# When the 64-bit weights of a gated layer are decoded: blocks moved between attention, expert 0 and experts 1 to 5

## The chip, the core and the metric

One core of a Trainium2 chip runs the whole program in one launch: attention, a mixture of experts, a gated feed-forward layer. The metric is the time of the launch in microseconds on the device. Three runs of the kernel before took 854.21, 855.8 and 856.52 us; the median is 855.8.

## The reference

For 4 batches of 8 heads, 576 positions and 64 columns a head, causal attention with a bias from running sums of `s`; its output, 2304 tokens of 512, goes to a top-1 mixture of eight experts (512 to 1024 to 512, relu), and that to an RMS norm and a gated layer of width 1536, all in float32 but for three weights:

```python
logits = x @ w_gate                      # mixture: one expert a token
h = np.maximum(xe @ w1[e], 0.0); ye = h @ w2[e]
out[mask] = gate_w[mask, None] * ye
xn = x / rms * rms_g                     # gated layer
g = xn @ w_gate                          # w_gate, w_val, w_out are float64
return ((g / (1 + np.exp(-g))) * (xn @ w_val) @ w_out).astype(np.float32)
```

The three weights of the gated layer reach the chip as 64-bit floats, 12 blocks (f = 0 to 11) of 128 x 512 words each. No engine reads them: a block is loaded as pairs of 32-bit words and decoded with shifts and masks.

## The kernel before

TensorE, VectorE, ScalarE and SyncE's DMA queue run in an order that the program writes out; each engine takes its instructions one after the other and waits on semaphores. GpSimd's order in attention and in the experts is the scheduler's.

**Attention** (`attention`). 16 head pairs p go through S (scores), X (exp), T (transposes), V (times values), W (copies to vp) and O (output and routing logits). All are laid into a plan by a time, ten units a pair, and emitted in the order of these times; other work has times of its own. After a batch (four pairs) `route` picks the expert of each token in some forty steps: VectorE finds the one-hot oh, TensorE ranks the tokens (rk), GpSimd scatters rows to xs with five indirect DMAs. The empty `yield 1` steps in it only let time pass in the plan.

**Weights of experts.** A float32 weight is split in a high part (a cast, `split` L728, ScalarE, or VectorE with `by_v`) and the rest (a subtraction; L743 on GpSimd for expert 0, L754 on VectorE for the others, one split late, `rest`). An expert has eight pieces of 512 KB, loaded by `feed` into one ring of four buffers (`staging`), through which the 64-bit blocks go as well. Expert 0's eight are split in attention at the times `PIECES`.

**Decoding** (`decoding` L1207) has five steps: shift, or, clear the sign (VectorE with `eng`, ScalarE's Abs without), scale, shift and or: L1212, L1213, L1214 or L1215, L1216, L1217. Of w_out, blocks 4 to 9 are decoded in attention (`out_load`, `out_first`, `out_last`, `out_keep`, the last storing 32-bit words to `wo32` in HBM), blocks 10 and 11 in expert 0 (`moe` L1007, into the one buffer `dw`). Of w_gate and w_val, blocks 0 and 1 are decoded in `glu_head`, a generator whose steps stand between the blocks of experts 6 and 7; the others in the gated layer.

**Experts** (`moe`). Expert s has eight blocks f of a first product (L891; h is written by ScalarE L894, its rest by VectorE L895), then four column blocks c of a second (L914), three passes each. Between them stand splits for the next expert, the turning of its rows (x_transpose), the norm of the expert before (`finish`) and the stores. In expert 0 the last batch's route runs on (`rank`).

**The gated layer** (`glu`, `glu_rest`), from 437 us on, is bound by TensorE and is not changed but for where its first blocks come from.

Of the kernel before, what the change touches and what calls it, by code (L numbers as in the profile page):

```python
# [19 lines left out]
E = 8  # L20
# [447 lines left out]
def route(k, b):  # L468
    nc, R = k.nc, k.rpool
    yield 1  # L470
    xt, lp = k.xt, k.lp
    sh = (128, 5, E)

    def t3(nm, dt=F32):
        return R.tile([128, 5, E], dt, name=f"{nm}{b}", tag=nm)

    def t2(nm, dt=F32):
        return R.tile([128, 5], dt, name=f"{nm}{b}", tag=nm)

    def up(x):  # L480
        return x.unsqueeze(2).broadcast_to(sh)

    w8 = k.w8.unsqueeze(1).broadcast_to(sh)
    base = k.base.unsqueeze(1).broadcast_to(sh)
    V = nc.vector
    lg, eq, dl, ex, ob, r1 = (t3(n) for n in ("lg", "eq", "dl", "ex", "ob", "r1"))
    mx, km, se, bt, rs = (t2(n) for n in ("mx", "km", "se", "bt", "rs"))
    oh, ix = t3("oh", BF16), t2("ix", U32)
    yield 1
    V.tensor_reduce(lg, lp, axis=AX.X, op=ALU.add)  # L490
    yield 1
    V.tensor_reduce(mx, lg, axis=AX.X, op=ALU.max)
    yield 1
    V.tensor_tensor(eq, lg, up(mx), op=ALU.is_ge)
    yield 1
    V.tensor_tensor(dl, lg, up(mx), op=ALU.subtract)
    yield 1
    V.tensor_tensor(eq, eq, k.w8v, op=ALU.mult)
    nc.scalar.activation(ex, dl, AF.Exp)
    yield 1  # L500
    V.tensor_reduce(km, eq, axis=AX.X, op=ALU.max)
    yield 1
    V.tensor_tensor(oh, up(km), w8, op=ALU.is_equal)
    yield 1
    for _ in range(3 if b < B - 1 else 0):
        yield 1
    ps = k.psum.tile([128, 48], F32, name=f"rk{b}", tag="b")
    rk = ps[:, 0:40].rearrange("p (t e) -> p t e", t=5)
    nc.tensor.matmul(rk, k.tri, oh, start=True, stop=False)
    for t in range(4):  # L510
        nc.tensor.matmul(rk[:, t + 1:5, :], k.ones, oh[:, t:t + 1, :].broadcast_to((128, 4 - t, E)), start=False, stop=t == 3)
    for t in range(5):
        nc.tensor.matmul(ps[:, 40:48], k.ones, oh[:, t, :], start=t == 0, stop=t == 4)
    yield 1
    V.tensor_tensor(ob, oh, base, op=ALU.mult)
    yield 1
    V.tensor_reduce(bt, ob, axis=AX.X, op=ALU.add)
    yield 1
    V.tensor_reduce(se, ex, axis=AX.X, op=ALU.add)
    yield 1  # L520
    V.tensor_scalar(xt[:, :, DM], k.tid, float(b * S), None, op0=ALU.add)
    yield 1
    V.tensor_scalar(se, se, 1e-9, None, op0=ALU.add)
    yield 1
    V.reciprocal(xt[:, :, DM + 1], se)
    yield 1
    V.tensor_tensor(r1, rk, oh, op=ALU.mult)
    yield 1
    V.tensor_reduce(rs, r1, axis=AX.X, op=ALU.add)
    yield 1  # L530
    V.tensor_tensor(ix, bt, rs, op=ALU.add)
    yield 1
    V.tensor_tensor(k.base, ps[:, 40:48], k.base, op=ALU.add)
    yield 1
    for t in range(5):
        n = 128 if t < 4 else 64
        yield 1
        i = nc.gpsimd.indirect_dma_start(
            out=k.xs, out_offset=bass.IndirectOffsetOnAxis(ap=ix[0:n, t:t + 1], axis=0),
            in_=xt[0:n, t, :], in_offset=None,  # L540
        )
        of_rows(k, "placed", in_turn(k, i).ins, k.filled)
        k.placed.append(i.ins)
    if b == B - 2:
        V.tensor_scalar(k.na, k.base[0:1, 0:1], float(NA), None, op0=ALU.min)
        V.tensor_scalar(k.base[:, 0:1], k.base[:, 0:1], float(NA), None, op0=ALU.max)
    if b == B - 1:
        for _ in order_experts(k):
            yield 1
# [73 lines left out]
MASK = -9.7  # L623
ROUTE = (35.2, 0.22)
FR = 2
PIECES = (81.8, 84.0, 91.8, 94.0, 159.0, 161.7, 165.3, 167.1)
EARLY_AT = (152.2, 165.25, 170.2, 170.3)
EARLY_P, EARLY_OUT = 9, 6
FILL = (12.6, 12.7, 12.8, 22.6, 22.7, 22.8, 32.5, 32.6)


def attention(k):
    k.st, k.todo, k.turn, k.half_done = {}, [], [], None
    with ExitStack() as es:
# [46 lines left out]
        for n in range(EARLY_OUT):  # L681
            at = 10 * (EARLY_P + n)
            add(at - (1.6, 5.0)[n] if n < 2 else at - 5.8, out_load, k, 4 + n)
            add(at + 6.3, out_first, k, 4 + n, k.nc.vector)
            add(at + 14.0, out_last, k, 4 + n)
            add(at + 16.4, out_keep, k, 4 + n)
        for n in (EARLY_OUT - 2, EARLY_OUT - 1):
# [12 lines left out]
        k.turn = []  # L700


RSTEPS = 40


PLACE = ((6, 7, 4, 5), (0, 1, 2, 3))
# [12 lines left out]
def feed(k, n=1):  # L719
    for _ in range(n):  # L720
        if k.order:
            s, u, q = k.order.pop(0)
            raw = staging(k, [2, 512], F32)
            src = (k.w1, k.w2)[u // 2]
            src = src[0, u % 2] if s == 0 else src[bass.ds(who(k, s), 1), u % 2].rearrange("e p q n -> (e p) q n")
            k.nc.sync.dma_start(out=raw, in_=src[:, q:q + 2, :])
            k.staged.append((s, u, q, raw))


def split(k, n=1, refill=True, by_v=False):  # L730
    nc = k.nc
    for _ in range(n):
        if k.staged:
            s, u, q, raw = k.staged.pop(0)
            if q == 0:
                new_unit(k, s, u)
            w = k.wt[s, u][:, q:q + 2]
            if by_v:
                nc.vector.tensor_copy(w[:, :, 0, :], raw)
            else:  # L740
                nc.scalar.copy(w[:, :, 0, :], raw)  # L741
            if s == 0:
                in_turn(k, nc.gpsimd.tensor_tensor(w[:, :, 1, :], raw, w[:, :, 0, :].bitcast(F32), op=ALU.subtract))  # L743
            else:
                rest(k)
                k.half_done = (w, raw)
            if refill:
                feed(k)
# [10 lines left out]
    k.early[f] = raw_load(k, 2, f)  # L759


def out_first(k, f, eng=None):
    for step in decoding(k, k.early[f], eng=eng)[0:3]:
        step()


def out_last(k, f, pool=None):
    if pool:
        done = k.early[-1] = pool.tile([128, 2 * CM], U32, name=f"dw{f}", tag="sq")[:, 0:512]
    else:  # L770
        done = k.early[-1] = new_raw(k).rearrange("p d two -> p (d two)")[:, 0:512]
    for step in decoding(k, k.early.pop(f), done)[3:5]:
        step()


def out_keep(k, f):
    k.nc.sync.dma_start(out=k.wo32[f // 2 - 2][:, f % 2, :], in_=k.early[-1].bitcast(F32))


STG = 4  # L780
# [207 lines left out]
def moe(k, close):  # L988
# [4 lines left out]
            next(k.last, None)  # L993

    k.order = [(s, u, q) for s in range(1, E) for u in range(4) for q in (0, 2)]
    late = range(4 + EARLY_OUT, NF)
    for f in late:
        out_load(k, f)
    row = ids(k, k.x[0], EARLY)
    keep_ids(k, row, 0)  # L1000
    rank(RANK[0])
    for f in range(8):
        gemm1(k, 0, f, NA)
        rank(RANK[f + 1])
        if f == 3:
            load_late(k)
        if f > 2 and f < 7:  # L1007
            (out_first, out_last)[f % 2 - 1](k, late[(f - 3) // 2], *((), (k.mpool,))[f % 2 - 1])
        if f > 4 and f % 2:
            out_keep(k, late[(f - 5) // 2])  # L1010
    load_x(k, 1)
    feed(k, STG - 1)
    first = tiles_of(CAP[0])
# [34 lines left out]
    for s in range(1, E):  # L1048
# [22 lines left out]
            next(head, None)  # L1071
        for c in range(4):
            gemm2(k, s, c, n)
            if c == 1:
                split(k)
            if not last:
# [156 lines left out]


def w_parts(k, f):
    return [k.raw[f, m].bitcast(F32)[:, :, n] for m in range(2) for n in (1, 0)]


# [92 lines left out]
def glu_head(k):  # L1331
# [3 lines left out]

    V, G = k.nc.vector, k.nc.gpsimd
    k.raw, k.ps = {}, {}
    w_load(k, 0, 0)
    yield
    w_load(k, 0, 1)  # L1340
    yield
    w_load(k, 1, 0)
    dec(0, 0, 0)
    yield
    w_load(k, 1, 1)
    dec(0, 0, 1)
    for g in range(2):
        glu_load(k, g)
    yield
    dec(0, 0, 2)  # L1350
    yield
    dec(0, 0, 3)
    yield
    dec(0, 0, 4)
    yield
    w_cast(k, 0, 0)
    dec(0, 1, 0, 1)
    yield
    w_rest(k, 0, 0, G)
    dec(0, 1, 2)  # L1360
    yield
    dec(0, 1, 3, 4)
    yield
    for n in (1, 4):
        w_cast(k, 0, n)
    yield
    for n in (1, 4):
        w_rest(k, 0, n, G)
    yield
    x_cast(k, 0, "A11")  # L1370
    x_rest(k, 0, "A11", V)
    dec(1, 0, 0, 1)
    yield
    x_cast(k, 0, "A12")
    dec(1, 0, 2)
    x_rest(k, 0, "A12", V)
    dec(1, 0, 3, 4)
    yield
    x_cast(k, 0, "A21")
    x_rest(k, 0, "A21", V)  # L1380
    dec(1, 1, 0, 1)
    yield
    x_cast(k, 0, "A22")
    x_rest(k, 0, "A22", G)
    dec(1, 1, 2, 3, 4)
    yield


# [548 lines left out]
def block_kernel(ctx, tc, q, kk, v, s, w_gate, w1, w2, wg, wv, wo, rms_g, out):  # L1937
# [7 lines left out]
    k.tokd = k.dpool.tile([YCOL], F32, name="tokd")  # L1945
    k.hd = k.dpool.tile([NG, 128, NF, GT], F32, name="hd")
    k.cumd = k.dpool.tile([32, S], F32, name="cumd")
    k.wo32 = k.dpool.tile([NF // 2 - 2, 128, 2, 512], F32, name="wo32")
    k.psum = ctx.enter_context(tc.tile_pool(name="psa", bufs=8, space=bass.MemoryType.PSUM))
    k.w64 = (k.wg, k.wv, k.wo64)  # L1950
# [82 lines left out]
```

## Time and profile before

| | |
|---|---|
| median of three runs | 855.8 us (854.21 to 856.52) |
| the profiled execution | 860.85 us |
| its span, first to last instruction | 859.1 us |
| TensorE busy | 827.8 us, 96% |
| VectorE / ScalarE / GpSimd busy | 637.5 / 462.2 / 232.4 us |
| mean granted clock of TensorE | 0.989 |
| moved by DMA | 145.67 MB |

PE is TensorE's matmuls, PEld its weight loads, DVE VectorE, ACT ScalarE, POOL GpSimd, SPq SyncE's queue. Times of rows are from the span's start. The number in brackets at the end of a row is how long the engine stood idle before it, and who ended that. A clock of 1.00 is TensorE's upper level, 2.4 GHz, 0.50 the lower, 1.2 GHz. Attention takes the span to about 194 us, expert 0 to 242, experts 1 to 7 to 437, the gated layer the rest.

### The profile page before, as it was taken

To read this page: it belongs to the slowest core of one execution; us is meant where nothing else is said; L and a number is where in the kernel's file an instruction comes from. 1 tells how busy PE (TensorE), PEld (TensorE's weight loads), DVE (VectorE), ACT (ScalarE), POOL (GpSimd) and SP (SyncE) were. 2 spreads that over 40 slices of the span, in tenths; PEclk is the share of its full clock that TensorE was granted. 3 is DMA by queue.
4 is the path that set the end of the run, shared out by engine and by line. 5 is a ranking of instruction groups with operands and counts; after the bars stand their busy time and mean duration, and the time that the engine had idled before them with its cause. 6 is when DMAs were issued, how large, how long until landed. Compare 5 with 4: busy or idle time off the path is not lost.

```text
span 859.1 us, 15794 instructions
## 1 busy us (share of the span) xinstructions
PE 827.8 (96%) x5622; PEld 754.6 (88%) x5622; DVE 637.5 (74%) x1424; ACT 462.2 (54%) x1059; POOL 232.4 (27%) x251
## 2 busy tenths in 40 slices
PE   7999999988999999999999999999999999999994
PEld 4767666667899999999999999999999997899994
DVE  6657587956575567567789998888888968867881
ACT  6988888872656556566453434333333335454340
POOL 3425745262000000000130313444444443022120
PEclk9999999998999999999999999999999999999998
DMA  7999978262674665666645342333323264544510
GB/s 227 309 302 300 296 244 265 93 216 93 202 237 153 185 196 167 211 187 197 212 159 175 107 166 77 114 105 105 105 95 108 92 257 150 152 147 130 163 54 29
DMA packets 79324, 145.67 MB, mean 170 GB/s; under 512 B 7376, under 2 KB 44267, under 8 KB 79235
## 3 DMA queue, kind: packets, MB, share of 16 engines
q1 hardware_dynamic: 76275, 135.03, 50.1%
q0 software_dynamic: 2912, 9.46, 2.9%
q8 instruction: 46, 0.75, 0.4%
q14 instruction: 43, 0.35, 0.1%
q10 hardware_dynamic: 48, 0.07, 0.0%
HBM read 107.52 MB, written 37.02 MB: 168 GB/s over the span
## 4 chain that ended last, share of the span: by engine, by line
PE 86%; DVE 5%; DMA 3%; ACT 2%; issue 1%; POOL 1%; SPq 0%; POOLq 0%; DVEq 0%; ACTq 0%
PE gg L1285 30%; PE g L914 12%; PE gp L1750 10%; PE g L891 9%; PE go L1685 6%; PE s L307 4%; PE t L370 4%; PE pvy L416 4%; PE tl L444 2%; DMA in<-cumd 1%; PE sm L338 1%; PE xp L862 1%; DMA raw<-in_w 1%; PE r L963 1%; PE r L952 1%
## 5 line engine op out<-in xcount | busy, mean ns | idle before, releaser
L914 PE MATMUL g<-h,u 128*128 128x256 f32 (+7 forms) x768 | 110.5, 303 | 5.0 <-DVE h L895 4.7
L914 PEld LDWEIGHTS g<-h,u 128*128 128x128 f32 x768 | 105.6, 196 | 6.6 <-DVE h L895 5.6
L891 PE MATMUL g<-xt,u 128*128 128x256 f32 (+7 forms) x768 | 104.5, 295 | 0.0
L891 PEld LDWEIGHTS g<-xt,u 128*128 128x128 f32 x768 | 101.6, 189 | 0.9
L1262 POOL TENSOR_TENSOR ws<-raw,ws 128x512 fp32r<-128x512 f32 (+1 forms) x25 | 33.5, 1352 | 232.2 <-ACT ws L1257 232.2
L351 ACT ACTIVATE p<-sc,nm 128x128 f32<-128x128 f32 (+3 forms) x128 | 71.2, 580 | 6.7 <-DVE nm L295 6.7
L754 DVE TENSOR_TENSOR u<-raw,u 128x1024 fp32r<-128x1024 f32 x56 | 68.0, 1216 | 0.4 <-ACT u L741 0.4
L1285 PE MATMUL gg<-gx2a,ws 128*128 128x384 f32 x360 | 67.4, 335 | 0.6 <-DVE tmp L1307 0.6
L1285 PE MATMUL gg<-gx0a,ws 128*128 128x384 f32 x360 | 67.7, 336 | 0.0
L741 ACT CAST u<-raw 128x1024 fp32r<-128x1024 f32 x62 | 65.1, 1050 | 4.7 <-DMA raw<-in_w 2.4
L1285 PE MATMUL gg<-gx1a,ws 128*128 128x384 f32 x360 | 67.1, 335 | 0.0
L1285 PEld LDWEIGHTS gg<-gx2a,ws 128*128 128x128 f32 x360 | 62.8, 188 | 0.9 <-DVE tmp L1307 0.9
L1285 PEld LDWEIGHTS gg<-gx0a,ws 128*128 128x128 f32 x360 | 63.1, 188 | 0.0
L1285 PEld LDWEIGHTS gg<-gx1a,ws 128*128 128x128 f32 x360 | 62.7, 188 | 0.0
L1323 POOL TENSOR_TENSOR hs<-tmp,hs 128x384 f32<-128x384 f32 x27 | 30.3, 1124 | 106.2 <-ACT hs L1321 106.2
L403 ACT COPY pt<-t 128x512 f32<-128x512 f32 (+3 forms) x160 | 55.7, 454 | 3.0 <-PE t L370 2.2
L370 PE MATMUL t<-ident,p 128*128 128x128 f32 x400 | 52.1, 275 | 0.1
L370 PEld LDWEIGHTS t<-ident,p 128*128 128x128 f32 x400 | 44.5, 140 | 8.3 <-DVE nm L295 8.0
L1671 POOL DMA_INDIRECT out<-raw,oid x18 | 20.5, 1140 | 112.1 <-DVE raw L1772 64.6
L922 DVE TENSOR_TENSOR sq<-sq 128x256 f32<-128x256 f32 (+6 forms) x21 | 9.6, 459 | 53.0 <-ACT sq L921 53.0
L416 PE MATMUL pvy<-pt,vp 128*64 128x512 f32 (+4 forms) x320 | 47.5, 428 | 0.9 <-ACT pt L403 0.9
L916 ACT COPY y<-g 128x256 f32<-128x256 f32 (+7 forms) x32 | 12.6, 395 | 59.8 <-PE g L914 59.8
(392 smaller groups left out, 1833.7 us busy)
## 6 DMA issues: line engine op xcount, KB each, us to landing
raw<-in_w SPq DMA_DIRECT2D x64, 512.0 KB
hd<-hs SPq DMA_DIRECT2D x72, 192.0 KB
xs<-zrow SPq DMA_DIRECT2D x8, 771.0 KB
raw<-in_wo SPq DMA_DIRECT2D x12, 512.0 KB
raw<-in_wg SPq DMA_DIRECT2D x12, 512.0 KB
raw<-in_wv SPq DMA_DIRECT2D x12, 512.0 KB
vp<-in_v SPq DMA_DIRECT2D x16, 320.0 KB
in<-cumd SPq DMA_DIRECT2D x20, 256.0 KB
```

The source lines that it names most:

```text
L307: k.nc.tensor.matmul(ps[h], st.q[r, 128 * i:128 * i + 128], st.k[r, 0:w], start=True, stop=p >= BYPE)
L351: k.nc.scalar.activation(out, st.s[i, h][:, 0:w], AF.Exp, bias=st.nm[:, n:n + 1], scale=-1.0, accum_out=acc)
L370: nc.tensor.transpose(ps[:, off:off + 128], src[:, 128 * j:128 * j + 128], k.ident)
L403: nc.scalar.copy(b, a)
L416: nc.tensor.matmul(st.y[r, a - 64:512], st.v[:, h, j, :], k.pt[:, h, o:o + S - a], start=j == 0, stop=j == 4)
L741: nc.scalar.copy(w[:, :, 0, :], raw)
L754: k.nc.vector.tensor_tensor(w[:, :, 1, :], raw, w[:, :, 0, :].bitcast(F32), op=ALU.subtract)
L891: nc.tensor.matmul(ps[:, 0:n], w[:, f % 4, a, 128 * kc:128 * kc + 128], x[b][:, kc, 0:n], start=kc == 0 and i == 0, stop=kc == 3 and i == 2)
L914: nc.tensor.matmul(ps[:, 0:n], w[:, f % 4, a, 128 * c:128 * c + 128], k.h[b][:, f, 0:n], start=f == 0 and i == 0, stop=f == 7 and i == 2)
L1285: k.nc.tensor.matmul(k.ps[u, bank], w[:, a, 128 * c:128 * c + 128], x[:, b, GT * c:GT * c + GT], start=first and c == 0 and n == 0, stop=c ...
L1685: k.nc.tensor.matmul(k.acc[tau], c[:, a, 128 * t:128 * t + 128], w[:, b, :], start=f == 0 and i == 0, stop=f == NF - 1 and i == 2)
L1750: k.nc.tensor.matmul(k.acc[i, bank], t[:, a, j, :], item_weight(k, j, w, b), start=first and j == 0 and n == 0, stop=j == 5 and n == 2, sk ...
```

## The change

The twelve early blocks are decoded in other places. In attention five blocks of w_out (4 to 8) and not six; in expert 0 none; instead `feed` and the ring carry five blocks of 64-bit words, one in each of experts 1 to 5, decoded by `decode_words` around the first column blocks of the second product: w_out's 9, 10 and 11, and block 0 of w_gate and w_val, which is stored to a new tensor `wg32`. `glu_head` loads that as 32-bit words and decodes block 1 alone, with its steps in other places. Of expert 0's eight splits the last two move from the end of attention into its blocks f = 2 and 4, with their subtraction on VectorE. Batch 1's route gets seven more empty steps ahead of its rank matmuls.

```diff
-    for _ in range(3 if b < B - 1 else 0):
+    for _ in range((3, 10, 3, 0)[b]):            # route
-PIECES = (81.8, 84.0, 91.8, 94.0, 159.0, 161.7, 165.3, 167.1)
+PIECES = (81.8, 84.0, 91.8, 94.0, 159.0, 161.7)
-EARLY_P, EARLY_OUT = 9, 6
+EARLY_P, EARLY_OUT = 9, 5
-RSTEPS = 40
+RSTEPS = 47
             s, u, q = k.order.pop(0)             # feed
+            if s == E:
+                k.staged.append((s, u, q, raw_load(k, u, q)))
+                continue
-            if s == 0:                           # split
+            if s == 0 and u < 3:
                 in_turn(k, nc.gpsimd.tensor_tensor(...))
+def compact(k, raw, out):
+    for step in decoding(k, raw, out.rearrange("p d two -> p (d two)")[:, 0:512])[3:5]:
+        step()
+def keep_words(k, m, f, t):
+    out = k.wo32[f // 2 - 2][:, f % 2, :] if m == 2 else k.wg32[:, m, :]
+    k.nc.sync.dma_start(out=out, in_=t.bitcast(F32).rearrange("p d two -> p (d two)")[:, 0:512])
+def decode_words(k):
+    s, m, f, raw = k.staged.pop(0)
+    for step in decoding(k, raw)[0:3]:
+        step()
+    yield
+    rest(k)
+    compact(k, raw, raw)
+    keep_words(k, m, f, raw)
+    feed(k)
+    yield
-    late = range(4 + EARLY_OUT, NF)              # moe
-    for f in late:
-        out_load(k, f)
+    words = [(E, 2, f) for f in range(4 + EARLY_OUT, NF)] + [(E, 0, 0), (E, 1, 0)]
+    for n, item in enumerate(words):
+        k.order.insert(WORDS_AT + 9 * n, item)   # WORDS_AT = 12
+    chain = iter(())
-        if f > 2 and f < 7:
-            (out_first, out_last)[f % 2 - 1](k, late[(f - 3) // 2], ...)
-        if f > 4 and f % 2:
-            out_keep(k, late[(f - 5) // 2])
+        if f in (2, 4):
+            split(k, 1, False)
+        elif f == 5:
+            rest(k)
             gemm2(k, s, c, n)
+            next(chain, None)
             ...
             split(k)
+            if c == 0 and s <= len(words):
+                chain = decode_words(k)
+                next(chain)
-    w_load(k, 0, 0)                              # glu_head
-    yield
-    w_load(k, 0, 1)
+    k.flat = staging(k, [2, 512], F32)
+    k.nc.sync.dma_start(out=k.flat, in_=k.wg32)
     yield
     w_load(k, 1, 0)
-    dec(0, 0, 0)
     yield
     w_load(k, 1, 1)
```

The rest of `glu_head` drops the steps of block 0 and brings those of block 1 (`dec(1, 0, ...)`, `dec(1, 1, ...)`) forward: its steps 0 and 1 come after f = 2 of expert 7, step 2 after f = 3, steps 3 and 4 after f = 5, each just after that block's h, and the value half at c = 0 and 1. GpSimd's subtractions for f = 0 come after f = 3 and f = 5.

## Rows read from the trace of the kernel before

**Rows 1.** The page's busy time of TensorE: us, share of the span, instructions.

```profile
PE 827.8 (96%) x5622; PEld 754.6 (88%) x5622; DVE 637.5 (74%) x1424; ACT 462.2 (54%) x1059; POOL 232.4 (27%) x251
```

**Rows 2.** Whom TensorE waited for: us in total, times, longest; whole span.

```profile
PE g L914 <- DVE h L895: 4.7, 2, 3.9
```

**Rows 3.** Stretches: length, busy us of each engine, granted clock, DMA share, GB/s.

```profile
191.10:194.30 3.20, 3.10 (x13) 2.90 (x14) 2.75 (x9) 1.15 (x5) 3.07 (x2) 0.50 0.28 108
...
211.60:218.20 6.60, 5.56 (x26) 5.56 (x27) 3.76 (x26) 0.76 (x2) 0.00 (x0) 0.50 0.36 114
```

**Rows 4.** Timeline (start, us, instruction, idle before): TensorE's ranks, batches 0 to 2.

```profile
75.92 0.19 PE L509 MATMUL rk<-oh,tri 128*128 128x40 bf16 x1 [0.28 <-DVE oh L503]
...
122.58 0.19 PE L509 MATMUL rk<-oh,tri 128*128 128x40 bf16 x1 [1.70 <-DVE oh L503]
...
167.90 0.19 PE L509 MATMUL rk<-oh,tri 128*128 128x40 bf16 x1 [1.55 <-DVE oh L503]
```

**Rows 5.** Timeline of VectorE, batch 2's route and a decoded block.

```profile
165.66 0.42 DVE L1212 TENSOR_SCALAR raw<-raw 128x512 uint32<-128x512 uint32 x1
```

**Rows 6.** Timeline of ScalarE, the end of attention.

```profile
188.38 2.17 ACT L741 CAST u<-raw 128x1024 fp32r<-128x1024 f32 x2 [2.19 <-issue]
```

**Rows 7.** Timeline of SyncE's queue, the end of attention.

```profile
181.67 1.22 SPq L726 DMA_DIRECT2D raw<-in_w  x2
```

**Rows 8.** Timeline of TensorE, the end of attention.

```profile
187.87 0.66 PE L444 MATMUL tl<-tg,vp 128*128 128x144 f32 x4
191.20 2.77 PE L444 MATMUL tl<-tg,vp 128*128 128x144 f32 x10 [2.68 <-ACT vp L428]
...
194.05 3.27 PE L891 MATMUL g<-xt,u 128*128 128x256 f32 x24
```

**Rows 9.** Timeline of TensorE, expert 0.

```profile
197.43 8.71 PE L891 MATMUL g<-xt,u 128*128 128x256 f32 x72
205.97 2.74 PE L914 MATMUL g<-h,u 128*128 128x256 f32 x22
212.64 8.69 PE L914 MATMUL g<-h,u 128*128 128x256 f32 x50 [3.93 <-DVE h L895]
```

**Rows 10.** Timelines of VectorE and of SyncE's queue, expert 0.

```profile
211.56 0.69 DVE L1217 SCALAR_TENSOR_TENSOR dw<-raw 128x512 uint32<-128x512 uint32 x1 [3.39 <-DMA wo<-dw]
...
208.25 4.36 SPq L777 DMA_DIRECT2D wo<-dw  x2
```

**Rows 11.** Timeline of TensorE, expert 7.

```profile
413.60 8.62 PE L891 MATMUL g<-xt,u 128*128 128x248 f32 x72
422.06 2.82 PE L914 MATMUL g<-h,u 128*128 128x248 f32 x19
...
426.37 10.63 PE L914 MATMUL g<-h,u 128*128 128x248 f32 x75 [0.23 <-ACT h L894]
```

**Rows 12.** Timeline of VectorE, expert 7.

```profile
424.12 0.42 DVE L1216 TENSOR_SCALAR raw<-raw 128x512 f32<-128x512 f32 x1
424.57 0.69 DVE L1217 SCALAR_TENSOR_TENSOR raw<-raw 128x512 uint32<-128x512 uint32 x1
...
426.35 0.42 DVE L895 SCALAR_TENSOR_TENSOR h<-g,h 128x248 fp32r<-128x248 f32 x1 [0.76 <-ACT h L894]
```

**Rows 13.** Stretches as in rows 3: expert 2.

```profile
271.00:300.60 29.60, 29.60 (x211) 28.75 (x210) 19.27 (x28) 17.52 (x35) 0.00 (x0) 1.00 0.60 185
```

**Rows 14.** Groups of the page: busy us, mean ns, idle before; a split's subtraction.

```profile
L754 DVE TENSOR_TENSOR u<-raw,u 128x1024 fp32r<-128x1024 f32 x56 | 68.0, 1216 | 0.4 <-ACT u L741 0.4
```

**Rows 15.** Timelines of VectorE and GpSimd, after expert 7.

```profile
439.00 1.66 DVE L1216 TENSOR_SCALAR raw<-raw 128x512 f32<-128x512 f32 x1 [0.87 <-ACT raw L1215]
...
438.54 1.84 POOL L1190 TENSOR_TENSOR gx0a<-ringa,gx0a 128x768 fp32r<-128x768 f32 x1 [11.31 <-ACT gx0a L1184]
```

**Rows 16.** Timelines of SyncE's queue and of ScalarE: a load and its split.

```profile
242.81 0.36 SPq L726 DMA_DIRECT2D raw<-in_w  x1
...
246.51 1.05 ACT L741 CAST u<-raw 128x1024 fp32r<-128x1024 f32 x1 [0.38 <-DMA raw<-in_w]
```

More of the change, by code (lines that the diff above doesn't have):

```diff
@@ L683, in attention @@
             add(at - (1.6, 5.0)[n] if n < 2 else at - 5.8, out_load, k, 4 + n)
-            add(at + 6.3, out_first, k, 4 + n, k.nc.vector)
+            add(at + 6.3, out_first, k, 4 + n)
             add(at + 14.0, out_last, k, 4 + n)
@@ L759, in out_load, with out_first, out_last, out_keep @@
     k.early[f] = raw_load(k, 2, f)
-def out_first(k, f, eng=None):
-    for step in decoding(k, k.early[f], eng=eng)[0:3]:
+def out_first(k, f):
+    for step in decoding(k, k.early[f], eng=k.nc.vector)[0:3]:
         step()
[L767 to L772, printed above, removed]
-        step()
-def out_keep(k, f):
-    k.nc.sync.dma_start(out=k.wo32[f // 2 - 2][:, f % 2, :], in_=k.early[-1].bitcast(F32))
+def out_last(k, f):
+    k.early[-1] = new_raw(k)
+    compact(k, k.early.pop(f), k.early[-1])
+def out_keep(k, f):
+    keep_words(k, 2, f, k.early[-1])
+def compact(k, raw, out):
+    for step in decoding(k, raw, out.rearrange("p d two -> p (d two)")[:, 0:512])[3:5]:
+        step()
+def keep_words(k, m, f, t):
[11 more added lines that the diff above has]
+    yield
 STG = 4
@@ L1006, in moe @@
             load_late(k)
-        if f > 2 and f < 7:
-            (out_first, out_last)[f % 2 - 1](k, late[(f - 3) // 2], *((), (k.mpool,))[f % 2 - 1])
-        if f > 4 and f % 2:
-            out_keep(k, late[(f - 5) // 2])
+        if f in (2, 4):
+            split(k, 1, False)
+        elif f == 5:
+            rest(k)
     load_x(k, 1)
@@ L1092, in moe @@
     k.tail = tail
+WORDS_AT = 6 + 6
 RANK = (9, 0, 10, 7, 0, 0, 0, 0, 3)
@@ L1235, in w_parts @@
 def w_parts(k, f):
+    if f == 0:
+        return k.flat[:, 0, :], None, k.flat[:, 1, :], None
     return [k.raw[f, m].bitcast(F32)[:, :, n] for m in range(2) for n in (1, 0)]
@@ L1337, in glu_head @@
     k.raw, k.ps = {}, {}
-    w_load(k, 0, 0)
-    yield
-    w_load(k, 0, 1)
+    k.flat = staging(k, [2, 512], F32)
+    k.nc.sync.dma_start(out=k.flat, in_=k.wg32)
     yield
     w_load(k, 1, 0)
-    dec(0, 0, 0)
     yield
     w_load(k, 1, 1)
-    dec(0, 0, 1)
+    yield
     for g in range(2):
@@ L1349, in glu_head @@
     yield
[L1350 to L1354, printed above, removed]
     yield
     w_cast(k, 0, 0)
-    dec(0, 1, 0, 1)
+    yield
+    dec(1, 0, 0, 1)
     yield
     w_rest(k, 0, 0, G)
-    dec(0, 1, 2)
-    yield
-    dec(0, 1, 3, 4)
+    dec(1, 0, 2)
     yield
@@ L1366, in glu_head @@
     yield
+    dec(1, 0, 3, 4)
     for n in (1, 4):
@@ L1369, in glu_head @@
     yield
+    yield
+    yield
     x_cast(k, 0, "A11")
     x_rest(k, 0, "A11", V)
-    dec(1, 0, 0, 1)
+    dec(1, 1, 0, 1)
     yield
     x_cast(k, 0, "A12")
-    dec(1, 0, 2)
+    dec(1, 1, 2)
     x_rest(k, 0, "A12", V)
-    dec(1, 0, 3, 4)
+    dec(1, 1, 3, 4)
     yield
@@ L1380, in glu_head @@
     x_rest(k, 0, "A21", V)
-    dec(1, 1, 0, 1)
     yield
@@ L1384, in glu_head @@
     x_rest(k, 0, "A22", G)
-    dec(1, 1, 2, 3, 4)
     yield
@@ L1947, in block_kernel @@
     k.cumd = k.dpool.tile([32, S], F32, name="cumd")
+    k.wg32 = k.dpool.tile([128, 2, 512], F32, name="wg32")
     k.wo32 = k.dpool.tile([NF // 2 - 2, 128, 2, 512], F32, name="wo32")
```

## The prediction

> **What bounds the kernel now.** I read the page first: TensorE is busy for 96% of the span [rows 1], so a change that leaves its matmuls alone can only win back what it stands still, and what it loses after standing still. Next, who TensorE waits for: the longest entry but the start of the program is the h of an expert, written by VectorE [rows 2]. Then TensorE's timeline around each of these, with VectorE, ScalarE and SyncE beside it, and last the granted clock by stretch. The reader is to see that all large holes lie in three places which this change touches (the end of attention, expert 0, expert 7), and that in two of them the clock of TensorE fell from its upper level (2.4 GHz) to the lower (1.2) once TensorE had stood still for over 2 us: 0.50 in 191.1 to 194.3 and in 211.6 to 218.2 [rows 3]. Such a hole costs more than its idle time.
>
> **The change, part by part** (durations from the profiled execution, 860.85 us, which is 0.6% above the median of 855.8).
>
> *Route of batch 1, seven empty steps before its rank matmuls.* TensorE waits 1.70 us for oh there; batch 0, whose route has no decoding beside it, waits 0.28 [rows 4]. VectorE's order is the same up to oh, so oh comes no sooner. What moves is TensorE's order: of the attention matmuls only those of one key block (V, 107.97 in the plan) lie between the old place 107.84 and the new one 109.38, some 0.3 us. They are done while TensorE would have waited. The scatter behind it is ordered on GpSimd behind the mask sums, and keeps its place. Gain 0.3, bounds 0 and 1.7.
>
> *Block 9 (the sixth of attention) leaves.* Its first three steps stand in VectorE's queue in the middle of batch 2's route (the first is shown [rows 5]; with the durations of rows 12 they are 0.42 + 0.69 + 0.42 = 1.5 us), and TensorE waits 1.55 us for that oh [rows 4]. Without them oh comes 1.5 us sooner, and what stays is batch 0's wait: 1.55 - 0.28 = 1.25 gained (bounds 0 and 1.55). Its load, its last two steps and its store leave SyncE and VectorE too. The two loads of expert 0 that were at 144.6 and 154.6 move to 134.6 and 144.6: the first takes the place and the wait of block 9's load, so it delays nothing that was not delayed.
>
> *Two splits leave the end of attention.* ScalarE stands until the weights land and then runs both casts, 2.17 us [rows 6]; the copy of vp is queued behind them, and the last ten O matmuls behind that: 2.68 us idle [rows 8]. The weights are late because SyncE issued them at 181.67, behind the rows x, which wait for batch 2's scatter [rows 7]. Without the casts vp follows the gate of x directly, its matmuls being done. The ten matmuls then start at 187.87 + 0.66 = 188.5, and at the upper clock take half of 2.77; expert 0 starts at about 190.0 and not at 194.05 [rows 8]. Gain 4.1; bounds 2.7 (the idle alone) and 4.1.
>
> *Expert 0: two decoded blocks out, two splits in.* Out of VectorE go 2 x (0.42 + 0.69 + 0.42 + 0.69) = 4.4 us [rows 12], and with them the one buffer dw: the second block's last step waited 3.39 us until the first block's store had landed, which SyncE had issued only at 208.25, behind the rows xl; h is queued behind it [rows 10]. TensorE stood still 3.93 us and then ran at the lower clock. The first three column blocks of the second product (22 + 50 = 72 matmuls) took from 205.97 to 212.64 + 8.69 = 221.33, that is 15.36; 72 matmuls of the same shape took 8.71 just before [rows 9]. Gain 15.36 - 8.71 = 6.65, lower bound the idle time, 3.93. In come two casts on ScalarE (2.17 / 2 each [rows 6]) and two subtractions of 1.22 on VectorE [rows 14], in blocks f = 2 to 5. VectorE has 2.0 us less to do than before; the cast delays an h by 1.1 us where TensorE has a free bank for some five more blocks. They are emitted at f = 4 and 5, and the second product, which comes to these weights half a column block after f = 7, follows two blocks later. Their loads are issued as in rows 7 or sooner, and now have 10 us more to land. If that cover were gone, each cast would cost 1.1. Taken: nothing. What is late next is h of f = 7, after TensorE's last block as always.
>
> *One block in each of experts 1 to 5.* Per expert 2.2 us of VectorE and at most 1.1 of ScalarE (a cast of twice the size takes that); in expert 2 VectorE is busy for 19.27 and ScalarE for 17.52 of 29.60 us, and TensorE for all of it [rows 13]. The first steps stand after the first column block of the second product, the last after the second. One new wait comes with it: SyncE's store of the block must land before the next load but one can take that buffer. A store took 211.56 - 208.25 = 3.3 us to land [rows 10], a load 246.51 - 242.81 = 3.7 [rows 16]. Behind it SyncE holds the next loads, the ids and the rows of the next expert, behind the late load ScalarE holds h of the next expert. But that split comes three splits later (about 7 us of matmuls), and h then has several free banks. Taken: nothing; bounds 0 and 3.3 an expert (2.2 + 1.1, nothing beside other work), no gain being possible, since nothing leaves here.
>
> *Expert 7: two decoded blocks out of four.* Its second product ran from 422.06 to 426.37 + 10.63 = 437.00, 14.94 us for 96 matmuls; at the first product's 8.62 / 72 they would take 11.49, so 3.45 are lost [rows 11]. VectorE does it: the last h ended at 426.77, behind two decoded blocks and the norm of expert 6 [rows 12]. With 2.2 less, it ends at about 424.6, just when TensorE comes to it. ScalarE still waits at the third step for VectorE, with four h behind it: I leave 0.5 of the loss. Gain 2.95, bounds 0.45 (below) and 3.45. The packed gate and value weights that are loaded instead were stored one and two experts earlier, so that load waits for nothing.
>
> Sum: 0.3 + 1.25 + 4.1 + 6.65 + 2.95 = 15.25. From the profiled execution's 860.85 this is 845.6; the same share of the median gives 840.6, the same difference 840.55. I take **840.5 us**. The lower bounds together (0 + 0 + 2.7 + 3.93 + 0.45 = 7.1) give 848.8, the upper ones (1.7 + 1.55 + 4.1 + 6.65 + 3.45 = 17.45) 838.35.
>
> **A rule that speaks against it.** Just after expert 7 a step of decoding that takes 0.42 us [rows 12] took 1.66 while GpSimd subtracted, and ended 0.28 us after GpSimd did [rows 15]. The new order puts GpSimd's two subtractions of f = 0 beside the last two steps of block 1 in expert 7, directly before the last two h. If both steps are slowed as in that row, by 1.24 each, 0.5 + 2.5 of expert 7's 3.45 stay lost, and 0.45 is gained: the lower bound above, and the first rival. The Trainium skill, "SBUF — State Buffer", section "Who interferes with whom", says that VectorE instructions in a two-port mode or with two SBUF inputs and GpSimd's reads exclude each other, and that the later one is blocked wholly. The trace agrees for this pair; by that rule the sum would be 843.
>
> **The rivals.**
> 1. *GpSimd blocks the decoding in expert 7, or another cover is thinner than it looks* (a cast in expert 0 or a block in an expert that costs TensorE 1 us). For it: rows 15, and that VectorE is busy for nearly all of expert 7's first product. Against: GpSimd's subtraction at f = 0 may be over by then. Time: 840.5 + 2.5 = 843 for expert 7 alone, up to 851 with an exposed microsecond in each of seven places.
> 2. *The holes were others' and come back*: xl or the rows of expert 1 arrive late because everything before them is sooner, the clock falls all the same, and expert 0 keeps its 6.65 and expert 7 its 2.95: 840.5 + 9.6 = 850; with the words' work in the experts exposed at 1 us each, 855, no change. For it: the scatter of batch 3 runs on GpSimd at its own pace, five indirect DMAs one after the other. Against: it starts sooner by the same 4 us as TensorE.
> 3. *Slower: the ring of four buffers in experts 1 to 5.* If the store's 3.3 and the reload's 3.7 us behind it come to TensorE in full, each of five experts pays 7.0, 35 in all: 840.5 + 35 = 875.5. It decides from 3.6 us an expert on (5 x 3.6 = 18 = 15.3 + 2.6). Against it: no split's wait for its data reached TensorE in these experts, which are busy throughout [rows 13].
> 4. *The change does not do what it says*: the seven steps move nothing but 0.3 us; that is already in the sum.
>
> **How the numbers follow.** Forecast (836.5 to 845) 0.62; rival 1 (845 to 851) 0.18; rival 2 with no change or little 0.11, of which 0.07 within 0.3% of before (853.2 to 858.4, about what a measurement of this kernel tells from no change); rival 3, 0.07; below 836.5, 0.02. The range 836.5 to 851 holds 0.80: its low end is the upper bounds' 838.35 less the spread of the runs, its high end the lower bounds' 848.8 and a few exposed microseconds. Faster 0.86, the same 0.07, slower 0.07.
>
> **What would show it.** In the changed kernel's trace: no wait of the O matmuls for vp at the end of attention, expert 0 starting some 6 us sooner (0.3 + 1.25 + 4.1); its second product's first 72 matmuls in about 8.7 us with the clock at 1.00; the rank wait of batch 2 near 0.3 and that of batch 1 still over 1; experts 1 to 5 as long as before; expert 7's second product near 12 us. It is wrong if TensorE waits for h in experts 1 to 6, if splits in expert 0 leave a hole before the second product, or if the clock is at the lower level after either place.

## The result: 842.1 us

Four runs of the changed kernel took 841.21 to 844.45 us, median 842.1; before 855.92 beside them, ratio 0.9846 (95% interval 0.9821 to 0.9871). Twice more, each time with before on the same chip, the ratio was 0.9810 (0.9781 to 0.9840) and 0.9829 (0.9807 to 0.9851). The first profiled execution of it took 841.21 us, with a span of 839.5. Lines of the changed kernel are twenty to thirty higher: h is L915 and L916, the two products L912 and L935, decoding L1239 to L1244.

The page after, TensorE's busy time and its clock in forty slices; [rows 1] answers to the first. It does the same 5622 matmuls, and only the last of the forty slices has a clock under 0.9 (a 9 stands for 90% or more):

```profile
PE 818.7 (98%) x5622; PEld 748.2 (89%) x5622; DVE 640.0 (76%) x1425; ACT 462.7 (55%) x1060; POOL 226.5 (27%) x249
PEclk9999999999999999999999999999999999999997
```

Whom TensorE waited for, as in [rows 2]. The h that cost 4.7 us is gone from the list, and so is vp; the longest wait behind the program's start is batch 1's oh:

```profile
PE s L307 <- DMA in<-in_k: 5.2, 1, 5.2
PE rk L509 <- DVE oh L503: 1.6, 2, 1.4
PE pvy L416 <- ACT pt L403: 0.7, 2, 0.4
```

TensorE's timeline after: the ranks of batches 1 and 2 [rows 4], the end of attention [rows 8], expert 0's start and its second product [rows 9], expert 7 [rows 11]:

```profile
120.83 0.19 PE L509 MATMUL rk<-oh,tri 128*128 128x40 bf16 x1 [1.37 <-DVE oh L503]
...
163.07 0.19 PE L509 MATMUL rk<-oh,tri 128*128 128x40 bf16 x1
...
182.30 1.88 PE L444 MATMUL tl<-tg,vp 128*128 128x144 f32 x14
...
184.16 3.08 PE L912 MATMUL g<-xt,u 128*128 128x256 f32 x24
...
195.86 8.62 PE L935 MATMUL g<-h,u 128*128 128x256 f32 x72
...
405.18 11.18 PE L935 MATMUL g<-h,u 128*128 128x248 f32 x96
```

No row but the first has a wait in brackets. The O matmuls (tl) run as one row of 14; the 72 matmuls that took 15.36 us take 8.62; expert 7's second product takes 11.18 and not 14.94. The clock in the stretches that answer to [rows 3], and TensorE in experts 1 to 7 (length, busy us of each engine, clock):

```profile
184.00:194.00 10.00, 10.00 (x95) 9.91 (x93) 8.13 (x34) 4.71 (x10) 3.27 (x4) 1.00 0.15 57
196.00:206.00 10.00, 10.00 (x88) 9.98 (x87) 5.55 (x41) 3.79 (x11) 0.06 (x1) 1.00 0.69 214
225.00:405.00 180.00, 180.00 (x1336) 175.84 (x1335) 130.82 (x201) 111.86 (x216) 2.06 (x3) 1.00 0.69 219
```

In 180 us of experts TensorE is never idle, with five blocks decoded beside it.

**By stages.** The two kernels were profiled again on one chip (before 856.05 us, after 843.01). Each stage ends at a matmul that both have; times and differences are in us, and the last column is the difference in the first pair of profiles:

| stage, from and to | forecast | before again | after again | difference | first two profiles |
|---|---|---|---|---|---|
| start to batch 0's rank | 0 | 76.12 | 77.54 | +1.42 | +0.16 |
| to batch 1's rank | -0.3 | 44.75 | 44.74 | -0.01 | -1.91 |
| to batch 2's rank | -1.25 | 43.74 | 42.25 | -1.49 | -3.08 |
| to expert 0's second product | -4.1 | 38.05 | 32.80 | -5.25 | -5.28 |
| to expert 1's first product | -6.65 | 32.77 | 26.59 | -6.18 | -6.75 |
| to the end of expert 7 | -2.95 | 196.24 | 193.91 | -2.33 | -3.77 |
| gated layer | 0 | 275.17 | 275.13 | -0.04 | +0.01 |
| rest of the span | 0 | 147.41 | 148.26 | +0.85 | +0.98 |

The five stages that were costed sum to 15.26, where 15.25 was forecast; the span falls by 13.0, since the first and the last stage give 2.3 back. The first stage's 1.42 is not of the change: the changed kernel's own two profiles differ there by 1.46 (76.08 and 77.54), and in the second of them TensorE waited 1.00 us for a load at 55 us, which it did not in the first. In the five costed stages these two profiles agree within 0.02 us; before's do not, which the first section of experiments takes up.

### The profile page after: what moved, and what is told of

Same layout as the page of the kernel before. It is cut to its first block, busy times and chain, and to the rows that moved or that the text cites. A ratio compares the mean times of both kernels' runs of the same rounds, so it can differ in the third digit from the quotient of the medians.

```text
span 839.5 us, 15787 instructions
## 1 busy us (share of the span) xinstructions
PE 818.7 (98%) x5622; PEld 748.2 (89%) x5622; DVE 640.0 (76%) x1425; ACT 462.7 (55%) x1060; POOL 226.5 (27%) x249
## 4 chain that ended last, share of the span: by engine, by line
PE 92%; DVE 3%; ACT 1%; DMA 1%; issue 1%; SPq 0%; POOL 0%; POOLq 0%; ACTq 0%; DVEq 0%
PE gg L1314 29%; PE g L935 12%; PE g L912 12%; PE gp L1772 10%; PE go L1707 6%; PE t L370 5%; PE s L307 5%; PE pvy L416 5%; PE tl L444 2%; PE sm L338 2%; PE xp L883 1%; DMA ringa<-ytd 1%; PE r L984 1%; PE r L973 1%; ACT pt L403 0%
## 5 line engine op out<-in xcount | busy, mean ns | idle before, releaser
L935 PE MATMUL g<-h,u 128*128 128x256 f32 (+7 forms) x768 | 105.0, 295 | 0.0
L912 PE MATMUL g<-xt,u 128*128 128x256 f32 (+7 forms) x768 | 104.2, 295 | 0.0
L912 PEld LDWEIGHTS g<-xt,u 128*128 128x128 f32 x768 | 101.4, 189 | 0.8
L935 PEld LDWEIGHTS g<-h,u 128*128 128x128 f32 x768 | 101.2, 189 | 0.5
L744 ACT CAST u<-raw 128x1024 fp32r<-128x1024 f32 x62 | 65.1, 1050 | 19.5 <-DMA raw<-in_w 19.5
L757 DVE TENSOR_TENSOR u<-raw,u 128x1024 fp32r<-128x1024 f32 x58 | 70.5, 1218 | 0.4 <-ACT u L744 0.4
L1332 ACT COPY tmp<-gg 128x384 f32<-128x384 f32 x27 | 13.0, 481 | 57.2 <-PE gg L1314 55.5
L1242 ACT ACTIVATE raw<-raw 128x512 f32<-128x512 f32 x31 | 21.2, 682 | 36.0 <-DVE raw L1240 35.9
```

What stands on the lines that cost most here:

```text
L757: k.nc.vector.tensor_tensor(w[:, :, 1, :], raw, w[:, :, 0, :].bitcast(F32), op=ALU.subtract)
L912: nc.tensor.matmul(ps[:, 0:n], w[:, f % 4, a, 128 * kc:128 * kc + 128], x[b][:, kc, 0:n], start=kc == 0 and i == 0, stop=kc == 3 and i == 2)
L935: nc.tensor.matmul(ps[:, 0:n], w[:, f % 4, a, 128 * c:128 * c + 128], k.h[b][:, f, 0:n], start=f == 0 and i == 0, stop=f == 7 and i == 2)
```

## The experiments

The studies used three sets of runs of before (medians 861.82, 857.55 and 857.9), so kernels of different studies are compared by their ratio to before.

### What belongs to single executions: before again

Edit: none. 

> The kernel before, profiled once more, for what belongs to single executions. Theory: the stalls of the S matmuls near 89 and 135 us and the stretches at the lower clock behind a rank wait come and go from execution to execution (the runs of before lie at 856 to 857 with a mean clock of 0.992 and at 861 to 862 with 0.986), so this profile differs from the first in these places by 1.5 to 5 us, and in none of the places that the change touches. Rival: they belong to the kernel; then the profile shows the same stalls at the same places.

856.05 us, span 854.3; the first profile's was 859.1. TensorE near 87 us, first in the first profile, then here; 16 S matmuls are due:

```profile
87.26 2.42 PE L307 MATMUL s<-in 64*128 64x128 f32 x14
90.64 0.91 PE L307 MATMUL s<-in 64*128 64x384 f32 x2 [0.96 <-ACT vp L428]
```

```profile
87.45 2.43 PE L307 MATMUL s<-in 64*128 64x128 f32 x16
```

In the first profile the last two waited for ScalarE's copy of vp, which came late: the copy had waited 2.97 us for TensorE, and 0.34 here. GpSimd scattered batch 0 beside it in both profiles; why the release came late in one is open. The same happened at 137 us, beside batch 1's scatter. The stages to batch 1's and batch 2's rank were 1.9 and 1.6 us longer by it, 3.5 together. For these stalls the theory holds: they are not of a kernel. The kernel with expert 7 undone (below), whose attention is the changed kernel's, had them in its profile, 46.59 and 44.13 us in these stages against 44.75 and 42.25; three profiles of the changed kernel had not. Nor do they come evenly: the profiles of all four kernels of the first study needed 46.4 to 46.6 us to batch 1's rank, and none of the eight of the later studies over 44.8. What the first study had in common is open.

That the two profiles of before agree wherever the change acts does not hold. In expert 7 they differ by 1.4 us: the second product's last 75 matmuls took 10.63 [rows 11] and here

```profile
418.16 2.81 PE L914 MATMUL g<-h,u 128*128 128x248 f32 x19
421.75 0.49 PE L914 MATMUL g<-h,u 128*128 128x248 f32 x2 [0.78 <-DVE h L895]
422.47 9.20 PE L914 MATMUL g<-h,u 128*128 128x248 f32 x75 [0.23 <-ACT h L894]
```

the same waits without the lower clock behind them (0.63 in 427 to 431 us of the first profile). The holes at vp and h of expert 0 were there again, of 2.9 and 4.4 us.

### Expert 0: the one buffer alone

```diff
-            ...(k, late[(f - 3) // 2], *((), (k.mpool,))[f % 2 - 1])
+            ...(k, late[(f - 3) // 2], *((k.mpool,) if f == 4 else ()))
```

> The kernel before, with one thing changed: the second block that is decoded in expert 0 writes its words into a buffer of the ring of four and not into the one buffer dw, so its last step no longer waits for the first block's store. All decoding stays where it was. Theory (the step 'expert 0' of the prediction): the wait of 3.39 us for that store is what holds h, makes TensorE stand 3.93 us and lets its clock fall; without it the first 72 matmuls of the second product take 8.7 to 9.5 us in place of 15.36, the clock stays at 1.00, and the time falls by 5.5 to 6.65 us, to some 849.5 us. Rival (the prediction's second): the rows xl or VectorE's decoding itself hold h; the hole stays at 2 us or more, the clock falls all the same, and the time falls by 0 to 2 us.

856.18 us against 861.82, ratio 0.9933 (0.9914 to 0.9952): 5.8 us by the ratio, with all decoding still in expert 0. TensorE's second product of expert 0:

```profile
205.98 2.74 PE L914 MATMUL g<-h,u 128*128 128x256 f32 x22
209.39 6.14 PE L914 MATMUL g<-h,u 128*128 128x256 f32 x50 [0.67 <-DVE h L895]
```

The 72 matmuls end at 215.53, so they take 9.55 us; the hole is 0.67 and not 3.93, and no lower clock follows. What held expert 0 was the wait of the second block's words for the first block's store, by one buffer. Neither xl nor VectorE's 4.4 us of decoding did, but for the 0.93 us by which 9.55 exceeds the changed kernel's 8.62. In its profile the stage from expert 0's second product to expert 1's first took 27.75 us, against 32.77 when before was profiled again (5.0 less) and 33.34 in the first profile.

### The end of attention: the splits alone, and put back

```diff
-PIECES = (81.8, 84.0, 91.8, 94.0, 159.0, 161.7, 165.3, 167.1)
+PIECES = (81.8, 84.0, 91.8, 94.0, 159.0, 161.7)
-            if s == 0:
+            if s == 0 and u < 3:
+        if f in (2, 4):
+            split(k, 1, False)
+        elif f == 5:
+            rest(k)
```

> The kernel before, with one thing changed: the last two splits of expert 0 stand in its f blocks (casts at f = 2 and 4, subtractions on VectorE at f = 4 and 5) and not at the end of attention. The two decoded blocks of expert 0 and the buffer dw stay. Theory (the step 'end of attention'): the last O matmuls no longer wait for vp, expert 0 starts 4.1 us sooner (5.2 by the traces), and the time falls by 2.7 to 5.2 us, to some 851.8; VectorE's 2.4 us more in expert 0 are hidden in the wait for dw. Rival (the prediction's second): what expert 0 waits for (xl behind batch 3's scatter, the store behind xl) keeps its own pace, so the hole of expert 0 grows by what the start gains, and the time falls by 0 to 1 us.

860.68 against 861.82, ratio 0.9986 (0.9967 to 1.0005): 1.2 us, by an interval that reaches no change, where 2.7 to 5.2 were expected. The vp hole is gone, but this profile has a loss that before's does not. Behind batch 2's rank, TensorE here and in the first profile of before:

```profile
168.78 0.19 PE L509 MATMUL rk<-oh,tri 128*128 128x40 bf16 x1 [1.56 <-DVE oh L503]
...
169.71 4.01 PE L307 MATMUL s<-in 64*128 64x128 f32 x16
```

```profile
168.83 2.43 PE L307 MATMUL s<-in 64*128 64x128 f32 x16
```

The wait is the same (1.55 in [rows 4]), but here the S matmuls behind it ran partly at the lower clock and took 1.58 longer. From batch 2's rank to the first product of expert 0 the profile gains 1.66, that is 3.2 but for this. The rival said that expert 0 would catch up; from there to expert 1's first product it took 45.63 against 45.26, only 0.4 of the gain. A little of the rival is seen: the stage of the second product grew from 33.34 to 33.93, with a wait of 1.43 us for ScalarE's h that before does not have. The rest of the gap to 1.2 us is open.

The same edit taken back, from the changed kernel, where no block 9 stands in attention: 

> The changed kernel with the two late splits of expert 0 put back to the end of attention. Theory (the step 'end of attention', 4.1, bounds 2.7 and 4.1): the last O matmuls wait for vp again, the clock falls, expert 0 starts 4 us later, and the time rises by 2.7 to 5.2 us. Rival: as in the kernel before with the splits moved alone, which gained 1.1 us only, expert 0 catches most of it up, and the time rises by 0 to 1.5 us.

845.19 us (843.8 to 846.56, 5 runs) against 843.01 (842.13 to 843.91): 2.2 us. TensorE at vp, and ScalarE's two casts ahead of it:

```profile
186.06 1.49 PE L444 MATMUL tl<-tg,vp 128*128 128x144 f32 x10 [1.71 <-ACT vp L428]
```

```profile
183.20 2.20 ACT L744 CAST u<-raw 128x1024 fp32r<-128x1024 f32 x2 [1.12 <-DMA raw<-in_w]
```

The hole is 1.71 and no lower clock follows (1.00 in 186 to 192 us). When before was profiled again it was 2.86, with SyncE's queue as follows (rows x stand ahead of these in both), and VectorE's own cast of a weight waiting for the first of these loads:

```profile
187.95 1.52 PE L444 MATMUL tl<-tg,vp 128*128 128x144 f32 x10 [2.86 <-ACT vp L428]
```

```profile
177.28 0.41 SPq L726 DMA_DIRECT2D raw<-in_w  x1
177.79 0.37 SPq L777 DMA_DIRECT2D wo<-raw  x1
178.22 1.05 SPq L726 DMA_DIRECT2D raw<-in_w  x2
```

```profile
182.67 0.70 DVE L739 CAST u<-raw 128x1024 fp32r<-128x1024 f32 x1 [4.49 <-DMA raw<-in_w]
```

In the kernel with the splits put back it reads

```profile
177.50 0.93 SPq L729 DMA_DIRECT2D raw<-in_w  x2
```

With block 9 a load of expert 0 more and block 9's store stand behind rows x and ahead of the two loads that the late splits wait for. Counted from batch 2's rank, the two loads are issued 0.57 us later with block 9 (13.61 against 13.04), and ScalarE's casts start 1.77 later (20.51 against 18.74). VectorE's cast holds lp as well, for which TensorE waits 0.40. From batch 2's rank to expert 0's second product the three kernels take 38.05 (before again), 35.29 (splits put back) and 32.80 us (after again): 2.49 of the 5.25 go with the splits, and 2.76 with block 9, some 1.2 of the hole and the clock's fall among them. So the 4.1 of the prediction is not the splits' alone. That block 9 acts here through SyncE's queue is read from these rows; no run took its load or its store away alone. The prediction moved that load and that store, but gave them no price.

### Block 9 back in attention

```diff
-EARLY_P, EARLY_OUT = 9, 5
+EARLY_P, EARLY_OUT = 9, 6
```

> The changed kernel with one thing undone: block 9 is decoded in attention again, its first steps in the middle of batch 2's route (and no such block in expert 1: four decoded blocks in experts 1 to 4). Theory (the step 'block 9'): TensorE waits about 1.55 us for batch 2's oh again, and the time rises by 1.25 us (0.9 to 1.6), to some 843.4 us. Rival: TensorE's early finish there is eaten by another wait later in attention, and the time stays within 0.4 us.

Ratio 0.9858 (0.9828 to 0.9887), against 0.9810 to 0.9846 of the changed kernel: 1 to 4 us more, which the intervals hardly tell from none. The profile tells more. The wait for oh is back at 1.56, and the 16 S matmuls behind it took

```profile
170.06 4.12 PE L307 MATMUL s<-in 64*128 64x128 f32 x16
```

with the clock at 0.57 in 170 to 174 us, where before had 1.00. So a wait of 1.55 us costs 1.5 in one execution (the 1.49 of the table) and 3.2 in another (1.56 + 1.69). And block 9 costs more than its wait: from batch 2's rank to expert 0's first product this profile took 24.68 us against 21.08, and of these 3.6 the clock behind the wait is 1.7; among the rest are two waits for ScalarE's copies pt, 0.72 and 0.58, whose cause was not tried.

### Expert 7

Edit: `glu_head` of before, no `(E, 0, 0), (E, 1, 0)` among the words. 

> The changed kernel with the part of expert 7 undone: four blocks are decoded in expert 7 as before, and no gate or value block in experts 4 and 5. Theory (the step 'expert 7'): the second product of expert 7 takes about 14.9 us again in place of 11.2 and the time rises by 2.95 to 3.8 us, to some 845.5 us. Rival (GpSimd's lock on VectorE, the prediction's first): the changed order already pays most of it, so undoing it costs 0 to 0.5 us.

Ratio 0.9876 (0.9848 to 0.9905), by which it is 2.6 to 5.7 us above the changed kernel, whose three ratios are 0.9810 to 0.9846. TensorE's second product of expert 7:

```profile
410.90 2.80 PE L935 MATMUL g<-h,u 128*128 128x248 f32 x19
414.48 0.49 PE L935 MATMUL g<-h,u 128*128 128x248 f32 x2 [0.78 <-DVE h L916]
415.20 9.21 PE L935 MATMUL g<-h,u 128*128 128x248 f32 x75 [0.23 <-ACT h L915]
```

It ends at 424.41: 13.51 us, and 11.18 in the changed kernel. By the profile the part is worth 2.33, a little under what the ratios say. For the rival, VectorE and GpSimd in the changed kernel's expert 7:

```profile
405.10 0.84 DVE L1243 TENSOR_SCALAR raw<-raw 128x512 f32<-128x512 f32 x1
```

```profile
404.22 1.43 POOL L1291 TENSOR_TENSOR ws<-raw,ws 128x256 fp32r<-128x256 f32 x2 [4.73 <-ACT ws L1286]
```

The step that takes 0.42 alone [rows 12] took 0.84 beside GpSimd. The Trainium skill, "SBUF — State Buffer", section "Who interferes with whom", has a VectorE instruction in a two-port mode, which a TENSOR_SCALAR can be in, and GpSimd exclude each other, and the trace agrees by this 0.42 us. But only this one step met GpSimd; the last h still ended at 407.31 and TensorE did not wait for it, so the rival's price was nothing. There was little to spare: where it waits for an h with this part undone, TensorE has done 19 of the 96 matmuls, and here it had done 19 by some 407.4 (an estimate: 405.18 and 19/96 of 11.18).

### The words in experts 1 to 5, doubled

```diff
-        k.order.insert(WORDS_AT + 9 * n, item)
+        k.order.insert(WORDS_AT + 10 * n, item)
+        k.order.insert(WORDS_AT + 10 * n + 3, (E, 3, n))   # stored to a spare tensor
 ...
-            if c == 0 and s <= len(words):
+            if c < 2 and s <= len(words):
```

> The changed kernel with its added work in experts 1 to 5 doubled: two blocks a expert are loaded, decoded and stored (the second into memory that nothing reads), five more loads, five more stores, 11 us more of VectorE. Theory (the prediction's step 'one block in each of experts 1 to 5' costs nothing): TensorE hides this too; the time stays within 0.5 us of the changed kernel. Rival (the prediction's third, the ring of four buffers): the cover was thin and a second block uses it up; each of five experts then shows a part of store and reload (3.3 + 3.7 us) as waits of TensorE for h or for weights: 5 us or more in all.

872.68 us against 843.01: 29.7 more, 5.9 an expert (5.3 to 7.5 in the profile). One block is free and the second, at this place, is not. SyncE's queue, VectorE, ScalarE and TensorE from expert 1 to expert 2:

```profile
248.54 0.33 SPq L786 DMA_DIRECT2D wo<-raw  x1
248.97 0.38 SPq L1227 DMA_DIRECT2D raw<-in_wg  x1
```

```profile
252.78 0.43 DVE L1240 TENSOR_SCALAR raw<-raw 128x512 uint32<-128x512 uint32 x1 [2.38 <-DMA raw<-in_wg]
```

```profile
254.03 0.67 ACT L1243 ACTIVATE raw<-raw 128x512 f32<-128x512 f32 x1 [5.45 <-DVE raw L1241]
```

```profile
255.67 0.40 PE L912 MATMUL g<-xt,u 128*128 128x304 f32 x1 [0.73 <-ACT xt L886]
258.47 3.91 PE L912 MATMUL g<-xt,u 128*128 128x304 f32 x14 [2.40 <-DVE xt L887]
```

The first block's store waits for VectorE's last step; the second block's load stands behind it on SyncE and lands at 252.78; VectorE's shift and ScalarE's Abs wait for it; behind Abs stand ScalarE's copies of xt, the next expert's turned rows, and VectorE's part of xt comes later still, behind the block's last two steps (256.88 to 258.03); TensorE has nothing else. Over the five experts it waits 6.5 us for ScalarE's xt and 11.9 for VectorE's. Then the clock is at 0.50 (259 to 264 us). The start of this is the third rival's queue, with the load of words and not of weights; its 7.0 us an expert is near the 5.9, but it had neither VectorE's steps nor the clock in it. In the changed kernel ScalarE's splits wait for loads too, 19.5 us in all in 225 to 405 us, up to 3.0 at once, and none of it reaches TensorE, which is busy for all of this stretch.

### Batch 1's wait, and a faster kernel

```diff
-            add(at + 6.3, out_first, k, 4 + n)
+            add(at + (7.3 if n == 1 else 6.3), out_first, k, 4 + n)      # block 5 later
-    for _ in range((3, 10, 3, 0)[b]):
+    for _ in range((3, 3, 3, 0)[b]):                                     # the steps out
```

The changed kernel as their measure: 

> The changed kernel itself, unchanged, on the chip and beside the runs of before that the next three use. Theory (the prediction's sum of 15.25, less what the ratio 0.9846 already showed): 13 to 15 us below before on any chip. Rival: part of the gain in the traces (3.4 us of S matmuls that stood still while batch 0's and batch 1's rows were scattered) belongs to single executions and not to the change; then its profile shows those stalls near 89 and 135 us again, and the gain is 10 to 12 us.

 843.06 us (842.27 to 844.13) against 857.55, 14.5 less; its profile has no stall near 89 or 135. Again, with the third study: 

> The changed kernel again, as the measure for the two kernels made from it in this study: 842 to 844 us on the chip of the study before; on the chip of the first study, by the ratio, some 845. Its clock should not fall before the end of the span in most executions; where batch 1's wait of 1.37 us lowers it, some 2 us more.

 843.01 us.

The seven steps out: 

> The changed kernel with the seven empty steps of batch 1's route taken out again. Theory (the prediction's first term): TensorE waits 1.70 in place of 1.37 us, and the time rises by 0.3 us, not told from no change; no more than 0.35 us can come of the order of TensorE. Rival: the longer wait is followed by a stretch at the lower clock more often, and the time rises by 1 to 2 us.

 843.53 us. The six runs fall in two groups, 841.92 to 842.47 and 844.59 to 844.81. The profiled one is of the upper; TensorE, and its clock in the stretch behind:

```profile
121.79 0.19 PE L509 MATMUL rk<-oh,tri 128*128 128x40 bf16 x1 [1.71 <-DVE oh L503]
```

```profile
122.00:127.00 5.00, 5.00 (x36) 2.73 (x32) 3.89 (x22) 2.51 (x10) 2.52 (x3) 0.66 0.96 269
```

When before was profiled again, a wait of 1.71 at this place was followed by no loss. The seven steps, then, gain nothing in the order of the work: the stage to batch 1's rank is 44.76 us here and 44.75 with them. They take 0.34 off a wait behind which the clock sometimes falls. Of the five profiles without the steps (1.69 to 1.71), two show slow S matmuls behind it, and of the seven with a wait of 1.35 to 1.37 none does.

Block 5 later, the steps kept: 

> The changed kernel with the first three steps of block 5 moved 1.0 us later in attention's plan, so that they stand behind batch 1's oh on VectorE and no longer in the middle of its route (as block 9's stood in batch 2's). Theory (the step 'block 9' applied to batch 1): TensorE's wait there falls from 1.37 to about 0.3 us, as batch 0's, and the time falls by 1.1 us against the changed kernel; by up to 2.7 on the mean if that wait, like that of batch 2 in the kernel with block 9 put back, is sometimes followed by a stretch at the lower clock (16 S matmuls took 4.12 us in place of 2.43). Rival: oh of batch 1 waits for other work of VectorE (its sc and nm), and nothing moves.

 841.0 us (840.22 to 842.76, 5 runs) against 843.06. The wait is gone:

```profile
119.24 0.19 PE L509 MATMUL rk<-oh,tri 128*128 128x40 bf16 x1
```

Both: 

> Both: block 5's first steps 1.0 us later and batch 1's seven empty steps taken out. Theory: as oh comes 1.1 to 1.5 us sooner, the rank matmuls at their old place wait 0.2 to 0.4 us, as batch 0's; 0.8 to 1.1 us below the changed kernel, and 0.3 above the kernel that keeps the seven steps, which no measurement here tells apart. Rival: as for that kernel, nothing moves.

 841.62 us, with a wait of 0.16. Decoding in the middle of the route was the cause for batch 1 as for batch 2. The stages, 44.75 and 42.25 in the changed kernel beside them, are 43.33 and 42.74 with block 5 later and 43.22 and 42.77 with both: 1.4 to 1.5 gained to batch 1's rank and 0.5 given back to batch 2's, 0.9 to 1.0 in all, near what the theory said. By the medians the first is 2.1 us faster than the changed kernel, the fastest here, but not all of this is shown to be the edit's: of the 3.0 us between the profiled executions 1.8 stand before batch 0's rank (75.91 against 77.67), which the edit does not touch. Its ratio to before is 0.9793 (0.9763 to 0.9823), and these intervals overlap.

## Why the prediction was right, point by point

*Route of batch 1.* Right that little moves, wrong that 0.3 stays: the wait fell from 1.71 to 1.37 and the stage is as long as before (-0.01). What the steps may be worth is a lower risk of the clock's fall, which the prediction did not price; two profiles of five against none of seven point that way and do not prove it.

*Block 9.* 1.25 forecast, 1.49 measured to batch 2's rank, by the cause named: its first steps in the route. That batch 0's wait of 0.28 would stay was wrong; batch 2's is nil. Two things were not in this step: the clock behind the wait, and what block 9 costs behind batch 2's rank, 2.76 by the profiles.

*Two splits.* 4.1 forecast, 5.25 measured in the stage, but the step put all of it to the splits. Put back alone they cost 2.2 by the medians and 2.49 in the profile, under the step's lower bound of 2.7; moved alone, with block 9 in place, they gained 1.2 (3.2 by the profile, but for a loss elsewhere). The mechanism (casts, vp, the last O matmuls) is there; by the rows the hole and the lower clock were as large as they were because the weights came later with block 9. The sum took the lower clock for the last ten O matmuls alone (2.77). That is so in the first profile; when before was profiled again these ten took 1.52 and the fall came behind them, in expert 0's first product (0.57 in 189 to 193 us), whose start lies 13.12 before the second product's, against 11.92 in the first profile and 11.72 after.

*Expert 0.* 6.65 forecast, 6.18 measured, and 5.0 of it by the buffer alone (in profiles; 5.8 by the ratio, 4.1 to 7.4). The idle time was 3.93; the rest is the clock behind it, as the prediction put it. The splits that came in cost TensorE nothing: the first product's 96 matmuls and the 72 behind run without a wait.

*The words.* Nothing forecast, nothing measured: from expert 1's first product on, the experts' lengths are 30.77, 29.57, 29.25, 28.48 and 27.81 us in the changed kernel's second profile and each within 0.01 of this in before's first. The doubled run shows that the cover ends before a second block.

*Expert 7.* 2.95 forecast from the first profile, where 3.77 was gained; 2.33 where the clock does not fall behind h. Of the 0.5 that the step left, nothing stayed (11.18 against 11.49). GpSimd did slow one step of VectorE (0.84 for 0.42), and it cost TensorE nothing.

*The total.* That the sum was right to 0.01 is luck: three terms were 0.3 to 0.6 too high and two 0.2 and 1.2 too low, and between block 9 and the splits the gain was divided wrongly. The median came 1.6 above the forecast. The span's end, from the last matmul on, is 0.8 to 1.0 longer in both pairs of profiles; why was not tried. The first pair of profiles shows 20.8 us in the same five stages, so 5.5 of it is of single executions.

## To carry to other kernels

Price a hole of TensorE as its idle time and, apart from that, what the clock takes behind it, and look at a second profile before either is put down to a change. When a late load is what an engine waits for, read the whole of the queue that issued it: a store of other work in front of it waits for an engine's last step, and holds everything behind. A free place beside TensorE is free for so many instructions: double the work once to see where it ends. And when two parts of a change meet in one stage, take each back alone before the stage's gain is shared out between them.

## What was not expected of the hardware

The same program's S matmuls beside the five indirect DMAs stood still in one execution and not in another (3.5 us in all), at the upper clock (1.00 in 84 to 93 and in 130 to 140 us); what decides is open. And a wait of 1.54 to 1.71 us for oh was followed by 16 S matmuls in 2.43 us in six cases and in 3.97 to 4.12 in four, with the same work at this place.
